# Linear attention feeding a gated product: one DRAM trip for the denominators' reciprocals, and nine pairs alone

## The chip, the cores and the metric

The kernel runs on one core of a Trainium2 chip. The metric is the device time of one execution in microseconds (us), the median of several runs. PE is TensorE, DVE is VectorE, ACT is ScalarE, POOL is GpSimd, SP is SyncE, which here only issues transfers (DMAs).

## The reference

```python
def phi(x):                                    # q, k: 8 batches x 8 heads x 576 x 64
    proj = np.einsum('bhsd,df->bhsf', x, w_phi)            # f = 128
    proj = proj - np.max(np.abs(proj), axis=-1, keepdims=True)
    return np.concatenate([np.exp(proj), np.exp(-proj)], axis=-1)
q_p, k_p = (phi(q), phi(k))
kv = np.einsum('bhsf,bhsd->bhfd', k_p, v)
z = np.sum(k_p, axis=2)
num = np.einsum('bhsf,bhfd->bhsd', q_p, kv)
den = np.einsum('bhsf,bhf->bhs', q_p, z)[..., None] + 1e-06
x = (num / den), heads side by side            # 4608 tokens x 512
out = ((x @ w_a) * (x @ w_b)) @ w_out          # w_a, w_b: 512 x 1536; w_out: 1536 x 512
```

## The kernel before

**Attention** goes over 32 pairs of heads (8 batches of 4 pairs; pair i is written b_pr, with i = 4 b + pr, so pair 8 is 2_0). For a pair, `project` makes the features: PE multiplies q into `pq` (two halves) and k into `pk`; DVE takes the largest magnitude `m` of k's rows and subtracts it (`d`), ACT takes both exponentials (`e`); for q, ACT copies `pq` to `p32`, POOL reduces over partitions (`mb`), DVE subtracts (`p`), ACT exponentiates (`eq`). 64 of a head's 576 keys are left over from the blocks of 128; they are done for two pairs together (`rk`, `e_r`, `m_r`, `d_r`). `kv_products` sums k's features times v into the bank `kv`; `z_products` puts the features' sums over the keys into a third part of the same bank, and `kv_out` copies it out (`back`). `turned_kv` transposes `back` on PE (`pt`) and DVE copies the result out (`kvh`). `num_products` then gives the numerators `pn`, which ACT copies to `x32`, and `den_products` the denominators `pd`. `pd` and `pt` take the same PSUM bank by turns while attention is alone. In `pd` each of four strips of 32 partitions holds 32 equal rows: one half of the times of one head.

**Sums over the keys.** For pairs from `ALONE` on, `summed` has DVE add the key blocks first (`two`, then `z` twice), and `z_products` needs 4 products; for the others it does 20 products on PE over the blocks themselves.

**Denominators.** `den_products` copies `pd` to `dn` and writes one row of each strip to DRAM (`den`). `reciprocals` runs in steps at later turns: read `den` back as 128 x 9 (`r`); add EPS and take the reciprocal on DVE (L306, L307); write it to DRAM (`rec`); read each head's row broadcast to 64 partitions (`rb`); multiply `x32` by `rb` on DVE (L316); write the result to DRAM (`xnorm`).

**The gated product** reads `xnorm`. Its first pass handles 6 of the 12 slices of the hidden dimension in 12 blocks of 384 tokens (`moe_block`; `pa`, `pb` and `po` are its sums, `h` the product of `pa` and `pb`, split in two for accuracy as `hh`, `hl`; `x` is split as `xh`, `xl`). The second pass (`winograd`) handles the rest from the same `xnorm`. The weights come in 64-bit form and are decoded in small steps by ACT and DVE (`w_a`, `w_b`, `w_o`: 18 tiles of 128 x 512, five DVE instructions each, spread over four steps).

**Order.** A planner counts turns, `TURNS` = 4 to a pair. Each unit of a pair is put at a turn: `SPREAD` for the first `ALONE` pairs, `PACKED` after them; the steps of `reciprocals` lie `rec_turns` after the denominators' products. Up to turn `begin` = 4 (`ALONE` + 1) attention is alone with the decoding (0.8 decode steps to a turn); after it there are 2.2 decode steps to a turn, and steps of the gated product run at `PACE0` and then `PACE` to a turn. PE's order of products is fixed as written while this lasts. `behind` and `issue_after` put an instruction behind the last load, or the last subtraction `d`, on its engine; SP issues all loads and stores in one queue, and an instruction that waits there holds up those after it.

Of the kernel before, what the change touches and what calls it, by code (L numbers as in the profile page):

```python
# [9 lines left out]
F32 = mybir.dt.float32  # L10
U32 = mybir.dt.uint32
F32R = mybir.dt.float32r
AF = mybir.ActivationFunctionType
# [5 lines left out]
P = 128  # L19
EPS = 1e-6  # L20


TURNS, ALONE = 4, 8
SPREAD = dict(turned_kv=9, kv_products=5, num_products=10, z_products=6, kv_out=6, den_products=11)
PACKED = dict(summed=2, turned_kv=5, kv_products=3, num_products=7, z_products=3, kv_out=3, den_products=7)
REC_TURNS0, REC_TURNS, X_TURNS = (2, 4, 5, 6, 8, 9), (1, 2, 2, 3, 4, 4), (2, 6)
DECODE_TURN, BLOCK_LAG = 3, 1
DECODE_ALONE, DECODE_BESIDE = 0.8, 2.2
PACE0, PACE, PACE0_TURNS = 0.36, 0.82, 21
# [14 lines left out]
def tile_kernel(ctx, tc, qP, km, kr, vm, vr, w_phi, eye, w_a, w_b, w_out, out):  # L44
# [13 lines left out]
    nc = tc.nc  # L58
    B, NPAIR, _, S = qP.shape
    H = 2 * NPAIR  # L60
    D, F = w_phi.shape
    DM, NT = out.shape
    DF = w_a.shape[0]
    NFULL = S // P
    HALF = S // 2
# [8 lines left out]
    xpool = xstack.enter_context(tc.tile_pool(name="xpool", bufs=1, side="right"))  # L74
    wpool = ctx.enter_context(tc.tile_pool(name="wpool", bufs=1))
    pstack = ExitStack()
    den = [dpool.tile([H, S], F32, name=f"den{b}") for b in range(B)]
    rec = [dpool.tile([H, S], F32, name=f"rec{b}") for b in range(B)]
    xnorm = [dpool.tile([DM, S], F32, name=f"xnorm{b}") for b in range(B)]
    part = dpool.tile([DM, NT], F32, name="part")  # L80
# [40 lines left out]
    def attention_consts(a1):  # L121
        w2 = a1.tile([P, F], F32, name="w2")
        for j in range(2):
            nc.scalar.dma_start(w2[j * D : (j + 1) * D, :], w_phi)
        ident = a1.tile([P, P], F32, name="ident")
        nc.scalar.dma_start(ident, eye)
        busy = a1.tile([P, 2 * S], F32, tag="eq", bufs=2, name="busy")[:, :WARM]
        nc.vector.memset(busy, 0.0)
        warm = duo("warm")
        for _ in range(WARM_TIMES):  # L130
            mm(warm[:, 0, :WARM], busy[:, :P], busy)
        ones = a1.tile([P, 3, D // 2], F32, name="ones")
        nc.vector.memset(ones, 1.0)
        nc.vector.memset(ones[D:, 1], 0.0)
        nc.vector.memset(ones[:D, 2], 0.0)
        return w2, ident, ones

    def split(hi, lo, src, eng_hi, eng_lo):

# [80 lines left out]
    def summed(b, pr, a1, a2, consts, st):  # L220

        u = f"{b}_{pr}"
        e, er = st["e", b, pr], st["er", b, pr // 2]
        two = a1.tile([P, 2, 2, 2 * F], F32, tag="two", name=f"two_{u}")
        ev = e.rearrange("p j c s f -> p j c (s f)")
        nc.vector.tensor_tensor(two, ev[:, :, 0:2], ev[:, :, 2:4], op=ALU.add)
        z = st["z", b, pr] = a2.tile([P, 2, 2 * F], F32, tag="z", bufs=1, name=f"z_{u}")
        nc.vector.tensor_tensor(z, two[:, :, 0], two[:, :, 1], op=ALU.add)
        rows = heads[pr % 2]
        rv = er.rearrange("p j c s f -> p j (c s f)")  # L230
        nc.vector.tensor_tensor(z[rows], z[rows], rv[rows], op=ALU.add)
# [38 lines left out]
    def num_products(b, pr, a1, a2, consts, st):  # L270
        u = f"{b}_{pr}"
        kvh, eq = st["kvh", b, pr], st["eq", b, pr]
        pn = duo(f"pn_{u}")
        for t in range(2):
            for s in range(2):
                for j in range(2):
                    mm(pn[heads[j], t, :HALF], kvh[:, s, heads[j]], eq[:, j, s, times[t]], start=(s == 0), stop=(s == 1))
        x32 = st["x", b, pr] = a2.tile([P, S], F32, tag="x32", bufs=3, name=f"x32_{u}")
        nc.scalar.copy(x32.rearrange("p (t n) -> p t n", t=2), pn[:, :, :HALF])

    def den_products(b, pr, a1, a2, consts, st):
        u = f"{b}_{pr}"
        kvh, eq = st["kvh", b, pr], st["eq", b, pr]
        pd = bank("pt", f"pd_{u}").rearrange("p s f -> p (s f)")
        for s in range(2):
            for j in range(2):
                for t in range(2):
                    mm(pd[strips[2 * j + t], :HALF], kvh[:, 2, strips[2 * j + s]], eq[:, j, s, times[t]], start=(s == 0), stop=(s == 1))
        dn = a2.tile([P, HALF], F32, tag="dn", bufs=1, name=f"dn_{u}")
        nc.scalar.copy(dn, pd[:, :HALF])  # L290
        rows = dn.rearrange("(g r) n -> g r n", r=P // 4)[:, 0]
        nc.sync.dma_start(den[b][2 * pr : 2 * pr + 2].rearrange("h (t n) -> (h t) n", t=2), rows)

    def behind(what, issue):

        with tc.issue_after(what[-1].ins):
            issue()

    def reciprocals(b, pr, a1, a2, st):

        n = 2 * S // P
        hs, rows = slice(2 * pr, 2 * pr + 2), slice(pr * P, (pr + 1) * P)
        r = a1.tile([P, n], F32, tag="rec", bufs=2, name=f"r_{b}_{pr}")
        behind(loads, lambda: nc.sync.dma_start(r, den[b][hs].rearrange("h (a n) -> (h a) n", n=n)))
        yield
        behind(marks, lambda: nc.vector.tensor_scalar_add(r, r, EPS))  # L306
        nc.vector.reciprocal(r, r)  # L307
        yield
        behind(loads, lambda: nc.sync.dma_start(rec[b][hs].rearrange("h (a n) -> (h a) n", n=n), r))
        yield  # L310
        rb = a2.tile([P, S], F32, tag="rb", bufs=1, name=f"rb_{b}_{pr}")
        for j in range(2):
            behind(loads, lambda: nc.sync.dma_start(rb[heads[j]], rec[b][2 * pr + j : 2 * pr + j + 1].broadcast_to([D, S])))
        yield
        x32 = st["x", b, pr]
        behind(marks, lambda: nc.vector.tensor_tensor(x32, x32, rb, op=ALU.mult))  # L316
        yield
        behind(loads, lambda: nc.sync.dma_start(xnorm[b][rows], x32))
        yield

    def attention_steps(pools, consts, st):

        stages, x_first = [], first_block_x()

        def once(f, *args):
            f(*args)
            yield

        def plan(order, unit, turns):
            for t in turns:  # L330
                stages.append((t, order, len(stages), unit))

        for i in range(B * NPAIR):
            b, pr = divmod(i, NPAIR)
            t0 = TURNS * i
            args = (b, pr, *pools, consts, st)
            at = SPREAD if i < ALONE else PACKED
            if i == ALONE - 1:
                at = dict(SPREAD, turned_kv=8, num_products=8, den_products=8)
            units = ((project, 0), (turned_kv, 0), (summed, 0), (kv_products, 0), (num_products, 0), (z_products, 0), (kv_out, 0))  # L340
            units += ((den_products, 0), (load_kq, -5), (load_v, -2))
            for order, (f, t) in enumerate(units):
                if f is not summed or i >= ALONE:
                    plan(order, once(f, *args), [t0 + at.get(f.__name__, t)])
            rec_turns = REC_TURNS0 if i < ALONE - 2 else REC_TURNS
            done = t0 + at["den_products"]
            plan(10, reciprocals(b, pr, *pools, st), [done + t for t in rec_turns])
            if b == 0:
                plan(11, x_first, [done + rec_turns[-1] + t for t in X_TURNS])
            if pr == NPAIR - 1:  # L350
                plan(12, b, [done + rec_turns[-1]])
        stages.sort(key=lambda x: x[:3])
        for turn_, group in itertools.groupby(stages, key=lambda x: x[0]):
            ready = None
            for *_, unit in group:
                if isinstance(unit, int):
                    ready = unit
                else:
                    next(unit, None)
            yield turn_, ready  # L360
# [142 lines left out]
    def first_block_x():  # L503

        for c in range(NCC):
            x32 = x_chunk(0, 0, c, xpool, 2)
            yield
            with tc.issue_after(acts[-1].ins), tc.issue_after(marks[-1].ins):
                x_make(0, 0, c, x32, xpool)
            yield  # L510
# [330 lines left out]
    def first_block(block):  # L841
        next(block)
        for f in range(NFS[0]):
            while (0, f, "b") not in weights:
                yield
            next(block)
            yield
        while (0, NFS[0] - 1, "o") not in weights:
            yield
        yield from block  # L850

    def home(f, nm):
# [4 lines left out]
    begin = TURNS * (ALONE + 1)  # L857
    with ExitStack() as c:
# [7 lines left out]
        decode_steps = placed(load_weights(units, pools[0]))  # L866
        for turn, ready in attention_steps(pools, consts, st):
            if ready is not None:
                at = max(turn + BLOCK_LAG, begin + 1)
                done, blocks[0] = blocks[0], (ready + 1) * S // T1  # L870
                tasks.setdefault(at, []).extend(moe_block(0, j) for j in range(done, blocks[0]))
                if ready == 0:
                    tasks[at][0] = first_block(tasks[at][0])
# [149 lines left out]
```

## Time and profile before

| | us |
|---|---|
| median of 3 runs | 1222.34 (1221.86 to 1228.75) |
| the profiled execution, whole time | 1230.14 |
| its span, first to last instruction | 1228.4 |
| PE busy | 1152.3 (94%) |
| DVE busy | 772.5 (63%) |
| ACT busy | 560.7 (46%) |
| POOL busy | 140.5 (11%) |

The span is what the views divide up; 1.7 us of the execution lie around it. Attention alone fills about the first 120 us, attention beside the gated product the stretch up to 580 us, the rest of the first pass lasts to about 820 us, and the second pass ends the program.

### The profile page before, as it was taken

To read this page: it belongs to the slowest core of one execution; us is meant where nothing else is said; L and a number is where in the kernel's file an instruction comes from. 1 tells how busy PE (TensorE), PEld (TensorE's weight loads), DVE (VectorE), ACT (ScalarE), POOL (GpSimd) and SP (SyncE) were. 2 spreads that over 40 slices of the span, in tenths; PEclk is the share of its full clock that TensorE was granted. 3 is DMA by queue.
4 is the path that set the end of the run, shared out by engine and by line. 5 is a ranking of instruction groups with operands and counts; after the bars stand their busy time and mean duration, and the time that the engine had idled before them with its cause. 6 is when DMAs were issued, how large, how long until landed. Compare 5 with 4: busy or idle time off the path is not lost.

```text
span 1228.4 us, 20607 instructions
## 1 busy us (share of the span) xinstructions
PE 1152.3 (94%) x7974; PEld 1027.5 (84%) x7974; DVE 772.5 (63%) x1411; ACT 560.7 (46%) x1050; POOL 140.5 (11%) x69
## 2 busy tenths in 40 slices
PE   7877886999999999999989999999999999999998
PEld 5544664688878788887989999999999999998997
DVE  6777789355555555554588722527768596867665
ACT  6765565345445444544355322424435353534332
POOL 4432213121212121211000000000000000000000
PEclk9998998899999999999999999999999999999999
DMA  6555544224232232312489410038576776768572
GB/s 203 154 172 162 156 146 141 96 68 127 79 117 93 84 121 65 123 48 82 158 292 312 137 46 25 28 118 308 177 268 213 221 247 215 252 201 284 174 236 97
DMA packets 103074, 191.73 MB, mean 156 GB/s; under 512 B 19520, under 2 KB 54720, under 8 KB 102976
## 3 DMA queue, kind: packets, MB, share of 16 engines
q1 hardware_dynamic: 102672, 190.28, 48.3%
q8 instruction: 63, 1.03, 0.4%
q14 instruction: 35, 0.29, 0.1%
q10 hardware_dynamic: 304, 0.13, 0.0%
HBM read 150.75 MB, written 39.62 MB: 155 GB/s over the span
## 4 chain that ended last, share of the span: by engine, by line
PE 68%; DMA 13%; DVE 12%; ACT 3%; issue 2%; SPq 1%; DVEq 0%; ACTq 0%
PE po L755 10%; PE pa L104 10%; PE pb L104 9%; PE pa L644 9%; PE pb L644 9%; PE po L104 9%; PE kv L104 4%; PE pn L104 3%; DMA rb<-rec 2%; PE pd L104 2%; DMA back_w<-kept_w 2%; DMA x<-xnorm 2%; PE pq L104 2%; DMA den<-dn 2%; DVE d L176 1%
## 5 line engine op out<-in xcount | busy, mean ns | idle before, releaser
L214 POOL PARTITION_ALL_REDUCE mb<-p x64 | 140.2, 2233 | 422.7 <-ACT p L208 329.6
L104 PE MATMUL po<-hh,w_o 128*128 128x384 f32 x576 | 156.8, 345 | 13.4 <-DVE w_o L426 8.6
L104 PE MATMUL pa<-xh,w_a 128*128 128x384 f32 x576 | 162.5, 343 | 0.7 <-DVE h L536 0.7
L104 PE MATMUL pb<-xh,w_b 128*128 128x384 f32 x576 | 158.9, 337 | 1.9 <-ACT o L566 1.7
L104 PEld LDWEIGHTS po<-hh,w_o 128*128 128x128 f32 x576 | 106.5, 192 | 20.6 <-DVE w_o L426 9.4
L104 PEld LDWEIGHTS pa<-xh,w_a 128*128 128x128 f32 x576 | 106.0, 190 | 6.2 <-ACT back L260 2.3
L104 PEld LDWEIGHTS pb<-xh,w_b 128*128 128x128 f32 x576 | 105.3, 188 | 2.6 <-ACT o L566 2.1
L104 PE MATMUL po<-hl,w_o 128*128 128x384 f32 x288 | 97.9, 341 | 1.1 <-DVE hl L141 1.1
L104 PE MATMUL pa<-xl,w_a 128*128 128x384 f32 x288 | 97.3, 338 | 0.0
L104 PE MATMUL pb<-xl,w_b 128*128 128x384 f32 x288 | 96.9, 336 | 0.0
L536 DVE TENSOR_TENSOR h<-pb,h 128x384 f32<-128x384 f32 x72 | 39.6, 550 | 84.2 <-PE pb L104 74.5
L175 DVE TENSOR_REDUCE m<-pk 128x8 f32<-128x1024 f32 x32 | 39.1, 1221 | 79.6 <-PE pk L104 79.5
L140 ACT CAST hh<-h 128x384 fp32r<-128x384 f32 x72 | 36.9, 512 | 111.3 <-DVE h L536 111.1
L755 PE MATMUL po<-hh_s,own_o 128*128 128x384 f32 x288 | 80.3, 336 | 0.3 <-ACT u L743 0.3
L104 PE MATMUL pn<-eq,kvh 128*64 128x288 f32 x512 | 70.1, 417 | 9.2 <-DVE kvh L268 7.9
L104 PE MATMUL kv<-e,v 128*64 128x256 f32 x512 | 66.7, 406 | 8.1 <-ACT back L260 4.6
L104 PEld LDWEIGHTS pn<-eq,kvh 128*64 128x64 f32 x512 | 38.6, 141 | 34.6 <-ACT p L208 7.0
L104 PEld LDWEIGHTS kv<-e,v 128*64 128x64 f32 x512 | 35.5, 143 | 31.4 <-issue 8.5
L755 PE MATMUL po<-hh_w,own_o 128*128 128x384 f32 x216 | 59.2, 334 | 0.0
L104 PE MATMUL pq<-q,w 64*128 64x288 f32 x256 | 48.0, 450 | 11.5 <-ACT p L196 6.8
L216 ACT ACTIVATE eq<-p 128x1152 f32<-128x1152 f32 x32 | 37.3, 1165 | 42.4 <-DVE p L215 37.7
L104 PEld LDWEIGHTS po<-hl,w_o 128*128 128x128 f32 x288 | 55.1, 191 | 1.4 <-DVE hl L141 1.4
(257 smaller groups left out, 2630.0 us busy)
## 6 DMA issues: line engine op xcount, KB each, us to landing
back_s<-kept_s SPq DMA_DIRECT2D x71, 512.0 KB
back_w<-kept_w SPq DMA_DIRECT2D x52, 512.0 KB
q<-in_qP SPq DMA_DIRECT2D x32, 288.0 KB
rb<-rec SPq DMA_DIRECT2D x64, 144.0 KB
xnorm<-x SPq DMA_DIRECT2D x32, 288.0 KB
part<-o SPq DMA_DIRECT2D x48, 192.0 KB
o<-part SPq DMA_DIRECT2D x24, 384.0 KB
out_x<-o SPq DMA_DIRECT2D x48, 192.0 KB
```

Of the source, the lines that this page charges most:

```text
L104: issue = lambda: nc.tensor.matmul(out, w, x, start=start, stop=stop, skip_group_check=True)
L140: (eng_hi.copy if eng_hi is nc.scalar else eng_hi.tensor_copy)(hi, src)
L175: nc.vector.tensor_reduce(out=m, in_=p, op=ALU.max, axis=AX.X, apply_absolute_value=True)
L176: marks.append(nc.vector.tensor_tensor(d, p, m.unsqueeze(3).broadcast_to([P, 2, n, F]), op=ALU.subtract))
L214: nc.gpsimd.partition_all_reduce(mb, p32[:, j], P, bass_isa.ReduceOp.absmax)
L216: nc.scalar.activation(eq[:, :, 0], p32, AF.Exp)
L536: nc.vector.tensor_tensor(h32, pab["b"], h32, op=ALU.mult)
L644: in_turn(lambda: nc.tensor.matmul(acc[to][i], w_, x_, skip_group_check=True, **at), u.startswith("1_0"))
L755: in_turn(lambda: nc.tensor.matmul(acc[m, to], w_, h_, skip_group_check=True, **f), False)
```

## The change

`dn` now takes EPS with its copy out of PSUM (an activation with a bias in place of a copy), and DVE takes the reciprocal of the whole tile `dn`, 128 x 288, in place. One row of each strip goes to DRAM as `rec` and comes back broadcast as `rb`; the trip of `den` out and back, the 128 x 9 tile and its two DVE instructions are gone. The steps lie at other turns: before a pair's `rb` is read, a period of four turns passes in the stretch alone (`REC_TURNS0`), one turn beside the gated product (`REC_TURNS`). `dn` and `rb` get two buffers in place of one. `ALONE` is 9 in place of 8, so that `begin` moves from turn 36 to turn 40, and the first block starts when `x_first` is done. `summed` runs only from pair 15 on (`SUM_FROM`); pairs 8 to 14 do 20 products for `z` in place of 4. `two` shares a buffer with `d`, three early `x32` tiles lie in another pool.

```diff
-TURNS, ALONE = 4, 8
+TURNS, ALONE, SUM_FROM = 4, 9, 15
-REC_TURNS0, REC_TURNS, X_TURNS = (2, 4, 5, 6, 8, 9), (1, 2, 2, 3, 4, 4), (2, 6)
+REC_TURNS0, REC_TURNS1, REC_TURNS, X_TURNS = (1, 3, 7, 10, 10), (1, 3, 6, 8, 8), (1, 2, 3, 5, 6), (5, 8)
+EARLY_X = (0, 2, 4)
...
-        two = a1.tile([P, 2, 2, 2 * F], F32, tag="two", name=f"two_{u}")
+        two = a1.tile([P, 2, 2, 2 * F], F32, tag=f"d{NFULL}", name=f"two_{u}")
...
-        dn = a2.tile([P, HALF], F32, tag="dn", bufs=1, name=f"dn_{u}")
-        nc.scalar.copy(dn, pd[:, :HALF])
-        rows = dn.rearrange("(g r) n -> g r n", r=P // 4)[:, 0]
-        nc.sync.dma_start(den[b][2 * pr : 2 * pr + 2].rearrange("h (t n) -> (h t) n", t=2), rows)
+        dn = st["dn", b, pr] = a2.tile([P, HALF], F32, tag="dn", name=f"dn_{u}")
+        nc.scalar.activation(dn, pd[:, :HALF], AF.Identity, bias=consts[3])
...
-        behind(loads, lambda: nc.sync.dma_start(r, den[b][hs].rearrange("h (a n) -> (h a) n", n=n)))
-        yield
-        behind(marks, lambda: nc.vector.tensor_scalar_add(r, r, EPS))
-        nc.vector.reciprocal(r, r)
-        yield
-        behind(loads, lambda: nc.sync.dma_start(rec[b][hs].rearrange("h (a n) -> (h a) n", n=n), r))
-        yield
-        rb = a2.tile([P, S], F32, tag="rb", bufs=1, name=f"rb_{b}_{pr}")
+        dn = st["dn", b, pr]
+        behind(marks, lambda: nc.vector.reciprocal(dn, dn))
+        yield
+        one = dn.rearrange("(g r) n -> g r n", r=P // 4)[:, 0]
+        behind(loads, lambda: nc.sync.dma_start(rec[b][2 * pr : 2 * pr + 2].rearrange("h (t n) -> (h t) n", t=2), one))
+        yield
+        rb = a2.tile([P, S], F32, tag="rb", name=f"rb_{b}_{pr}")
...
-                if f is not summed or i >= ALONE:
+                if f is not summed or i >= SUM_FROM:
-            rec_turns = REC_TURNS0 if i < ALONE - 2 else REC_TURNS
+            rec_turns = REC_TURNS0 if i < ALONE - 4 else REC_TURNS1 if i < ALONE - 2 else REC_TURNS
...
+        yield
         yield from block
...
-                at = max(turn + BLOCK_LAG, begin + 1)
+                at = max(turn + (BLOCK_LAG if ready else X_TURNS[-1] + 1), begin + 1)
```

DVE's queue around the projection of pair 5 (1_1), in the stretch alone, before (`x32_0_1` and `r_0_2` are of pairs 1 and 2):

```order
L175 TENSOR_REDUCE m_1_1_655<-pk_1_1_645 128x8
L176 TENSOR_TENSOR d_1_1_654<-pk_1_1_645,m_1_1_655 128x1024
L268 COPY kvh_0_3_683<-pt_0_3_679 128x384
L316 TENSOR_TENSOR x32_0_1_460<-x32_0_1_460,rb_0_1_696 128x576
L306 TENSOR_SCALAR r_0_2_699<-r_0_2_699 128x9
L307 RECIPROCAL r_0_2_699<-r_0_2_699 128x9
```

The same place with the change:

```order
L177 TENSOR_REDUCE m_1_1_640<-pk_1_1_630 128x8
L178 TENSOR_TENSOR d_1_1_639<-pk_1_1_630,m_1_1_640 128x1024
L305 RECIPROCAL dn_0_2_616<-dn_0_2_616 128x288
L270 COPY kvh_0_3_667<-pt_0_3_663 128x384
L315 TENSOR_TENSOR x32_0_0_338<-x32_0_0_338,rb_0_0_603 128x576
```

The reciprocal now stands ahead of the copy `kvh` (in the pairs with an even number it stands behind it), the two small instructions are gone, and the multiplication is of one pair earlier.

SP's queue in the same stretch before, with the two trips of pairs 0 and 1:

```order
L309 DMA rec0_76<-r_0_0_449 128x9
L313 DMA rb_0_0_574<-rec0_76 64x576 x2
L292 DMA den0_68<-dn_0_1_498 4x288
L304 DMA r_0_1_577<-den0_68 128x9
L150 DMA k32_1_2_630<-in_km 128x512
```

With the change, from the reads of pair 0's row on:

```order
L312 DMA rb_0_0_603<-rec0_68 64x576 x2
L165 DMA rv_1_2_718<-in_vr 128x256
L308 DMA rec0_68<-dn_0_1_491 4x288
L389 DMA raw_0_2_a_728<-in_w_a 128x1024
L152 DMA k32_1_3_741<-in_km 128x512
L154 DMA q32_1_3_743<-in_qP 128x576
L168 DMA v32_1_2_720<-in_vm 128x512
L312 DMA rb_0_1_722<-rec0_68 64x576 x2
```

A write and the read of the same row stand five rows apart there, where before the read of `den` followed its write at once.

DVE's queue at the last weight tile of the first pass, `w_0_5_o`, before; pair 14 (3_2) has just been projected:

```order
L307 RECIPROCAL r_3_0_2154<-r_3_0_2154 128x9
L215 TENSOR_TENSOR p32_3_2_2111<-p32_3_2_2111,mb_3_2_0_2146 128x576
L228 TENSOR_TENSOR z_3_2_2202<-two_3_2_2200 128x512
L415 TENSOR_SCALAR w_0_5_o_2108<-w_0_5_o_2108 128x512
L231 TENSOR_TENSOR z_3_2_2202<-z_3_2_2202,e_r_3_2_2142 64x512
L417 TENSOR_SCALAR w_0_5_o_2108<-w_0_5_o_2108 128x512
L422 SCALAR_TENSOR_TENSOR w_0_5_o_2108<-raw_0_5_o_2059,w_0_5_o_2108 128x512
L423 TENSOR_TENSOR w_0_5_o_2108<-w_0_5_o_2108,w_0_5_o_2157 128x512
L215 TENSOR_TENSOR p32_3_2_2111<-p32_3_2_2111,mb_3_2_1_2149 128x576
L316 TENSOR_TENSOR x32_3_0_2081<-x32_3_0_2081,rb_3_0_2207 128x576
L426 TENSOR_TENSOR w_0_5_o_2157<-w_0_5_o_2108 128x512
```

With the change, where pair 15 (3_3) has just been projected:

```order
L178 TENSOR_TENSOR d_3_3_2259<-pk_3_3_2250,m_3_3_2260 128x1024
L315 TENSOR_TENSOR x32_3_0_2026<-x32_3_0_2026,rb_3_0_2172 128x576
L305 RECIPROCAL dn_3_1_2234<-dn_3_1_2234 128x288
L421 SCALAR_TENSOR_TENSOR w_0_5_o_2175<-raw_0_5_o_2134,w_0_5_o_2175 128x512
L422 TENSOR_TENSOR w_0_5_o_2175<-w_0_5_o_2175,w_0_5_o_2179 128x512
L270 COPY kvh_3_2_2285<-pt_3_2_2281 128x384
L228 TENSOR_TENSOR two_3_3_2318<-e_3_3_2263 128x1024
L217 TENSOR_TENSOR p32_3_3_2245<-p32_3_3_2245,mb_3_3_0_2271 128x576
L425 TENSOR_TENSOR w_0_5_o_2179<-w_0_5_o_2175 128x512
```

The last weight tile stands one pair later; on PE the first output block `po` of the first block stands one pair later too, behind the transposition of pair 14 in place of pair 13.

## Rows read from the trace of the kernel before

**Rows 1.** Engines by stretch: us, PE, PEld, DVE, ACT, POOL busy, clock, DMA.

```profile
27.85:82.95 55.10, 46.62 (x607) 30.82 (x603) 40.38 (x61) 40.43 (x61) 24.06 (x11) 1.00 0.50 155
82.95:121.37 38.42, 28.21 (x278) 16.44 (x274) 27.78 (x48) 20.09 (x31) 9.17 (x5) 0.87 0.53 165
121.37:217.10 95.73, 71.68 (x553) 54.15 (x549) 80.75 (x132) 54.89 (x88) 22.69 (x10) 0.91 0.48 143
217.10:240.00 22.90, 22.90 (x158) 16.96 (x160) 6.24 (x9) 6.50 (x11) 4.26 (x2) 0.86 0.28 91
```

**Rows 2.** DVE's waits for DMA in the first three stretches: us, times, longest.

```profile
DVE x L316 <- DMA rb<-rec: 8.5, 3, 4.0
DVE r L306 <- DMA r<-den: 3.5, 2, 1.9
...
DVE r L306 <- DMA r<-den: 4.0, 3, 2.1
DVE x L316 <- DMA rb<-rec: 3.7, 2, 3.0
...
DVE x L316 <- DMA rb<-rec: 7.0, 4, 3.0
DVE r L306 <- DMA r<-den: 1.5, 1, 1.5
```

**Rows 3.** Waits of PE over the span: total, times, longest.

```profile
PE kv L104 <- DVE z L231: 8.8, 5, 3.4
PE po L104 <- DVE w_o L426: 8.6, 2, 4.8
PE pn L104 <- DVE kvh L268: 7.9, 6, 2.1
```

**Rows 4.** PE in order of time, attention alone: start, us, instruction, [wait before it].

```profile
52.78 2.16 PE L104 MATMUL pn<-eq,kvh 128*64 128x288 f32 x16
54.87 1.08 PE L104 MATMUL kv<-e,ones 128*32 128x128 f32 x32
...
55.98 1.15 PE L104 MATMUL pd<-eq,kvh 128*32 128x288 f32 x16
...
57.66 1.06 PE L104 MATMUL pk<-w,k 64*128 64x128 f32 x16
```

**Rows 5.** PE in order of time, beside the gated product: last weight, `z` by 4 products.

```profile
217.09 0.69 PE L104 MATMUL po<-hh,w_o 128*128 128x384 f32 x1 [3.74 <-DVE w_o L426]
...
285.43 0.43 PE L104 MATMUL kv<-z,ones 128*32 128x128 f32 x8
285.68 1.15 PE L104 MATMUL pd<-eq,kvh 128*32 128x288 f32 x16
...
366.18 0.42 PE L104 MATMUL kv<-z,ones 128*32 128x128 f32 x8 [1.99 <-DVE z L231]
```

**Rows 6.** DVE in order of time: two small instructions, each with the one behind it.

```profile
45.10 0.18 DVE L306 TENSOR_SCALAR r<-r 128x9 f32<-128x9 f32 x1
45.18 0.68 DVE L422 SCALAR_TENSOR_TENSOR w_a<-raw_a,w_a 128x512 f32<-128x512 uint32 x1
...
59.15 0.22 DVE L307 RECIPROCAL r<-r 128x9 f32<-128x9 f32 x1
59.28 0.37 DVE L415 TENSOR_SCALAR w_b<-w_b 128x512 uint32<-128x512 uint32 x1
```

**Rows 7.** DVE's groups up to 240 us: count, busy us, mean ns, idle before.

```profile
L215 DVE TENSOR_TENSOR p<-p,mb 128x576 f32<-128x576 f32 x31 | 22.9, 740 | 0.1
L316 DVE TENSOR_TENSOR x<-x,rb 128x576 f32<-128x576 f32 x14 | 11.0, 787 | 17.7 <-DMA rb<-rec 17.4 <-issue 0.3
L226 DVE TENSOR_TENSOR two<-e 128x1024 f32<-128x1024 f32 x8 | 9.5, 1194 | 0.0
L228 DVE TENSOR_TENSOR z<-two 128x512 f32<-128x512 f32 x8 | 5.4, 680 | 0.0
L231 DVE TENSOR_TENSOR z<-z,e_r 64x512 f32<-64x512 f32 x7 | 4.8, 680 | 0.1
```

More of the change, by code (lines that the diff above doesn't have):

```diff
@@ L76, in tile_kernel @@
     pstack = ExitStack()
-    den = [dpool.tile([H, S], F32, name=f"den{b}") for b in range(B)]
     rec = [dpool.tile([H, S], F32, name=f"rec{b}") for b in range(B)]
@@ L135, in attention_consts @@
         nc.vector.memset(ones[:D, 2], 0.0)
-        return w2, ident, ones
+        eps = a1.tile([P, 1], F32, name="eps")
+        nc.vector.memset(eps, EPS)
+        return w2, ident, ones, eps
     def split(hi, lo, src, eng_hi, eng_lo):
@@ L277, in num_products @@
                     mm(pn[heads[j], t, :HALF], kvh[:, s, heads[j]], eq[:, j, s, times[t]], start=(s == 0), stop=(s == 1))
-        x32 = st["x", b, pr] = a2.tile([P, S], F32, tag="x32", bufs=3, name=f"x32_{u}")
+        i = b * NPAIR + pr
+        place, bufs = (alone["early"], 2) if i in EARLY_X else (a2, 3)
+        x32 = st["x", b, pr] = place.tile([P, S], F32, tag="x32", bufs=bufs, name=f"x32_{u}")
         nc.scalar.copy(x32.rearrange("p (t n) -> p t n", t=2), pn[:, :, :HALF])
@@ L299, in reciprocals @@
     def reciprocals(b, pr, a1, a2, st):
-        n = 2 * S // P
-        hs, rows = slice(2 * pr, 2 * pr + 2), slice(pr * P, (pr + 1) * P)
-        r = a1.tile([P, n], F32, tag="rec", bufs=2, name=f"r_{b}_{pr}")
-        behind(loads, lambda: nc.sync.dma_start(r, den[b][hs].rearrange("h (a n) -> (h a) n", n=n)))
+        rows = slice(pr * P, (pr + 1) * P)
+        dn = st["dn", b, pr]
+        behind(marks, lambda: nc.vector.reciprocal(dn, dn))
         yield
-        behind(marks, lambda: nc.vector.tensor_scalar_add(r, r, EPS))
-        nc.vector.reciprocal(r, r)
+        one = dn.rearrange("(g r) n -> g r n", r=P // 4)[:, 0]
+        behind(loads, lambda: nc.sync.dma_start(rec[b][2 * pr : 2 * pr + 2].rearrange("h (t n) -> (h t) n", t=2), one))
         yield
-        behind(loads, lambda: nc.sync.dma_start(rec[b][hs].rearrange("h (a n) -> (h a) n", n=n), r))
-        yield
-        rb = a2.tile([P, S], F32, tag="rb", bufs=1, name=f"rb_{b}_{pr}")
+        rb = a2.tile([P, S], F32, tag="rb", name=f"rb_{b}_{pr}")
         for j in range(2):
@@ L505, in first_block_x @@
         for c in range(NCC):
-            x32 = x_chunk(0, 0, c, xpool, 2)
+            with tc.issue_after(loads[-1].ins):
+                x32 = x_chunk(0, 0, c, xpool, 2)
             yield
```

## The prediction

> **What bounds the kernel now.** I read the busy times by stretch first, then the waits of PE and DVE, then both engines in order of time where those waits lie. In all, PE is busy 1152.3 of 1228.4 us, so the end is set by PE's work and by what PE loses. The losses to look for lie ahead of 240 us. While attention is alone (27.85 to 82.95 us) five pairs take 55.10 us, 11.0 each, of which PE is busy 46.62 and DVE 40.38 [rows 1]: neither is full, and DVE stands 12.0 us waiting for the row of denominators (`r`) or of reciprocals (`rb`) to come back from DRAM [rows 2]. The reader should see that PE and DVE wait for each other by turns here: a pair's `m` and `d` on DVE need PE's `pk`, and PE's `pn` needs DVE's `kvh`. In the passage to the gated product (82.95 to 121.37 us) PE is busy 28.21 of 38.42 us, with 7.7 us of such DMA waits on DVE; beside the gated product (to 217.10 us) 71.68 of 95.73 us, with 8.5 us of them, and DVE is busy for 80.75 [rows 1, 2]. [...] That stretch ends with PE waiting for the last weight that DVE decodes, at 217.09 us [rows 5]; DVE's sums `z` and weights are PE's longest waits [rows 3]. From there to 240 us PE has no idle time [rows 1].
>
> So I follow the time at which that last weight is ready. It stands one pair later in the changed order, on DVE and on PE. The pair that PE has then done more is worth 46.62 / 5 = 9.3 us [rows 1]. Equal to before would be 217.1 + 9.3 = 226.4 us.
>
> **The reciprocal's price.** No row shows one of 288 columns; 32 of these now stand on DVE. The one of 9 columns lets the next instruction start after 0.13 us, the addition of 9 columns after 0.08 [rows 6]. The difference over 9 columns is 5.6 ns a column beyond an addition's; at about 1 ns for that (0.74 us for 576 columns with the fixed part [rows 7]) a column takes some 6.6 ns and 288 of them 1.9 us, with the fixed part 1.95 us. Bounds: if all that is extra in the small one is fixed, 288 columns take 0.3 + 0.15 = 0.45 us; if nothing in it is fixed, 288 x 0.13 / 9 = 4.2 us. I take 1.95, an estimate, since the additions of 9 columns show that a fixed part of some 0.07 exists. The two small instructions that go took 0.18 + 0.22 = 0.4 [rows 6], so a pair gains 1.55 us on DVE.
>
> The rows give about 6.6 ns a column. [...]
>
> **Part by part, stretch by stretch.** The trip of `den` and `r` goes, and `rb` is read four turns behind its write, or one beside the gated product; SP's rows between write and read are loads that wait for products long done. I cost the transfers at nothing: DVE's 28.2 us of DMA waits [rows 2] go, and what is late next is DVE itself, whose queue now holds the reciprocal. Queued behind it are, in the odd pairs alone, `kvh`, for which PE's `pn` waits, and everywhere the subtractions `p`, for which ACT's `eq` waits. The bias in ACT's copy of `pd` I cost at nothing, as the same elements pass. SP loses one transfer out and one in to a pair; POOL's queue is not touched.
>
> *Alone.* DVE had 40.38 / 5 = 8.1 us of work a pair, now 8.1 + 1.55 = 9.65, against PE's 9.3. In two pairs the loop runs from the even pair's `m` to the odd pair's `kvh` on DVE, then over PE from `pn` to the end of the next `pk`, 52.78 to 58.72 = 5.9 us [rows 4]. On DVE that is 19.3 less what stands behind the odd pair's `kvh`: a multiplication 0.79, two `p` 1.48 [rows 7] and about half a pair's decoding, some 1.2 by instructions of 0.68 [rows 6], 3.5 in all. 19.3 - 3.5 + 5.9 = 21.7, or 10.8 a pair; before it was 11.0. Six pairs: 65 us, up to 27.85 + 65 = 92.9.
>
> *Passage.* On DVE: 38.42 less 7.7 of DMA waits, less two pairs' `summed` at 1.19 + 0.68 + 0.68 = 2.55 [rows 7], plus two reciprocals at 1.55; on PE plus two pairs' `z`: 1.11 us with 20 products (54.87 to 55.98 [rows 4]) for 0.25 with 4 (285.43 to 285.68 [rows 5]), 0.86 each. That is 30.4 if DVE's part decides and 40.1 if nothing of the waits is won, since PE and ACT wait for each other there too. I take 36: 128.9 us.
>
> *Beside the gated product.* DVE's 80.75 us lose five `summed` (12.8) and gain 5 x 1.55 = 7.8, one early `two` of pair 15 (1.2), and lose 3.2 of the decode steps, which the four more turns alone have done at 0.8 a turn: about 2.6 us at 0.68 an instruction and five instructions to four steps [rows 6]. Sum: 74.3. Of DVE's 15.0 us idle, 8.5 were DMA waits [rows 1, 2]; 6.5 stay, and I add 2 because a DVE with less to do waits more for PE: 82.8. PE's own work there is 71.68 at a clock of 0.91, about 65 at full, plus 5 x 0.86 = 69.5: not the bound, but near enough that little more can be won. The weight is ready at 128.9 + 82.8 = 211.7 us, 14.7 ahead of 226.4.
>
> *Later.* The pairs from 15 on keep `summed`, with the reciprocal now ahead of it. PE waited for `z` five times, two of them after 240 us (366.18 is one [rows 5]); 1.55 more each is 3.1 us. The other fifteen such sums came early enough to show no wait, and I leave them at nothing; what hides them is a step of the gated product on PE between a pair's products. I add 1 us won from less time at the lower clock level. Sum: -14.7 + 3.1 - 1 = -12.6 us. The profiled execution, 1230.1 us, would become 1217.5; it stood 7.8 above the median of the three runs, so against that median the forecast is 1222.3 - 12.6 = **1210 us**.
>
> **Rivals.**
> *The order eats it.* The wait for DMA is only changed into a wait for the reciprocal ahead of `kvh` and `p`. For it: PE already waited 7.9 us for `kvh` [rows 3], and the last weight still stands behind a whole pair's work. Then 6 x 11.0 = 66, 40.1 and 74.3 + 15.0 = 89.3 give 223.3, and with the 3.1 later **1222**. Against it: those waits grew in pairs where DVE had just stood for DMA.
> [...]
> *The reciprocal is dear.* At 4.0 us, near the upper bound, DVE is the bound in every stretch: 13 x 2.05 = 26.7, and `z` comes 2 us later in 17 pairs, of which I count five as unhidden, 10: **1247**, slower than before. It decides from a price of about 2.65 us (12.6 over 18 places is 0.7) and makes it slower by over 1% from 3.3. Against it: the fixed part that the addition of 9 columns shows.
> *The reciprocal is cheap.* At 0.45 us PE is the bound alone: 6 x 9.3 = 55.8 for 65, passage 3 less, beside the gated product 69.5 + 9 = 78.5 for 82.8, nothing late afterwards: 20 us more won, **1190**.
> That the change doesn't do what it says I exclude: the order shows the trip gone and the reads behind.
>
> **How the numbers follow.** Forecast 0.42, its own range 1198 to 1217; the order 0.18; eight cycles 0.12; dear 0.13; cheap 0.15. A measurement of this kernel tells about 1% from no change. Faster by over 1% (under 1210.1): cheap 0.15 and the better part of the forecast 0.30, 0.45. Within 1%: the rest of the forecast 0.12 and the two rivals at 1219 to 1222, 0.29 together with a small part of the edges, 0.41. Slower: 0.14. The range goes from the cheap case to a little beyond the order's, 1190 to 1229, and leaves out the dear one.
>
> **What would show it.** The reciprocals of 128 x 288 at 1.8 to 2.1 us; no wait of DVE for `rb` worth naming; pairs alone 10.5 to 11 us apart, with PE waiting for `kvh` in the odd ones; PE's first `po` waiting for its last weight at 206 to 217 us; 0.86 us more of PE for each of pairs 8 to 14; waits for `z` gone there and longer from pair 15 on. The prediction is wrong if the reciprocal's price is not near 1.95 us, if the first `po` no longer waits and PE is full beside the gated product (then more is won), or if SP's queue holds back loads of k and q, which showed no such wait before.

## The result, and the profile after

| | before | after |
|---|---|---|
| median of 4 runs, us (lowest to highest) | 1223.42 (1221.86 to 1228.75) | 1209.43 (1205.79 to 1214.27) |
| ratio, 95% interval | 1 | 0.9881 [0.9834, 0.9927] |
| profiled execution, us; its span | 1230.1; 1228.4 | 1205.8; 1204.0 |
| TensorE clock, mean of the span | 0.983 | 0.991 |

Faster by 1.2%, with 1210 forecast. The two spans differ by 24.4 us and the medians by 14.0: the profile of before is of a run 6.7 us above its median, that of after of one 3.6 us below. Some 10 us of what the traces show is therefore not the change's, and the text below leans on stretches and medians rather than on the whole spans.

The stretches of after that answer to [rows 1], each ended at the same event: six pairs alone, passage, beside the gated product, and from the last weight to 226.4 us.

```profile
27.54:92.54 65.00, 57.02 (x730) 37.77 (x727) 57.92 (x70) 49.55 (x74) 27.43 (x13) 0.97 0.53 163
92.54:128.05 35.51, 26.35 (x282) 16.34 (x280) 26.41 (x36) 17.71 (x27) 8.99 (x4) 0.90 0.54 165
128.05:213.77 85.72, 72.86 (x734) 57.16 (x730) 74.01 (x109) 54.12 (x85) 21.92 (x10) 0.98 0.50 157
213.77:226.40 12.63, 12.63 (x101) 8.63 (x103) 2.04 (x4) 5.33 (x8) 0.00 (x0) 0.86 0.19 63
```

DVE shows no wait for a DMA of the reciprocals in the first three of them. Before had 25.3 us of such waits up to 217 us:

```profile
DVE x L316 <- DMA rb<-rec: 16.2, 8, 4.0
DVE r L306 <- DMA r<-den: 9.1, 6, 2.1
```

The waits of PE over the span of after, to [rows 3] (total, times, longest):

```profile
PE pn L104 <- DVE kvh L270: 11.6, 5, 3.9
...
PE po L104 <- DVE w_o L425: 5.2, 1, 5.2
...
PE kv L104 <- DVE z L233: 0.8, 1, 0.8
```

PE of after in order of time: an odd pair's `pn`, and the last weight, to [rows 5].

```profile
57.68 2.16 PE L104 MATMUL pn<-eq,kvh 128*64 128x288 f32 x16 [1.75 <-DVE kvh L270]
...
213.77 0.62 PE L104 MATMUL po<-hh,w_o 128*128 128x384 f32 x1 [5.19 <-DVE w_o L425]
```

DVE of after in order of time, ahead of that `pn`. The reciprocal stands between `d` and `kvh`, and the multiplication `x` of an earlier pair behind `kvh`.

```profile
52.71 1.22 DVE L177 TENSOR_REDUCE m<-pk 128x8 f32<-128x1024 f32 x1 [0.42 <-PE pk L104]
54.04 1.23 DVE L178 TENSOR_TENSOR d<-pk,m 128x1024 f32<-128x1024 f32 x1
55.18 1.94 DVE L305 RECIPROCAL dn<-dn 128x288 f32<-128x288 f32 x1
57.04 0.49 DVE L270 COPY kvh<-pt 128x384 f32<-128x384 f32 x1
57.45 1.83 DVE L315 TENSOR_TENSOR x<-x,rb 128x576 f32<-128x576 f32 x1
```

The last weight is ready at 213.77 us, against the 226.4 at which the two kernels would be even: 12.6 us ahead, 14.7 forecast. The rest of the difference between the traces comes later: the second pass begins at 816.35 us before and at 794.03 after, 22.3 us apart. The stretches from the last weight to there, first before, then after:

```profile
217.09:816.35 599.26, 586.39 (x4038) 517.87 (x4038) 317.97 (x575) 262.99 (x489) 72.46 (x34) 0.99 0.35 110
213.77:794.03 580.26, 573.38 (x3950) 510.73 (x3951) 331.83 (x550) 260.37 (x482) 68.87 (x32) 0.99 0.35 111
```

The second is 19.0 us shorter, of which the pair that PE has already done is 9.3. Of the 9.7 us left, 6.0 are idle time of PE (12.9 us before, 6.9 after). Some 3 are clock: in these stretches PE's granted clock stood at 0.50, its lower level, for 13.2 us before and 6.8 after, and at 1.00 otherwise. Work took 1.9 times as long at 0.50: 16 products of `kv` took 3.68 us at 217.70 us in before, 1.95 at 238.37. How much of the 9.7 us belongs to the change is open, since it is of the size of the 10 us by which the two profiled runs stray from their medians.

### The profile page after: what moved, and what is told of

The parts are those of the page before. It is cut to its first block, busy times and chain, and to the rows that moved or that the text cites. A ratio compares the mean times of both kernels' runs of the same rounds, so it can differ in the third digit from the quotient of the medians.

```text
span 1204.0 us, 20915 instructions
## 1 busy us (share of the span) xinstructions
PE 1149.0 (95%) x8198; PEld 1030.4 (86%) x8198; DVE 795.8 (66%) x1359; ACT 565.0 (47%) x1050; POOL 139.3 (12%) x69
## 4 chain that ended last, share of the span: by engine, by line
PE 70%; DVE 10%; DMA 5%; ACT 3%; issue 2%; SPq 0%; ACTq 0%; DVEq 0%
PE po L755 10%; PE pa L104 10%; PE po L104 10%; PE pb L104 10%; PE pa L644 9%; PE pb L644 9%; PE kv L104 4%; PE pn L104 3%; DMA x<-xnorm 2%; PE pd L104 2%; PE pq L104 2%; DMA back_w<-kept_w 1%; PE pk L104 1%; DVE dn L305 1%; DVE h L536 1%
## 5 line engine op out<-in xcount | busy, mean ns | idle before, releaser
L104 PE MATMUL pn<-eq,kvh 128*64 128x288 f32 x512 | 72.0, 426 | 14.5 <-DVE kvh L270 11.6
L305 DVE RECIPROCAL dn<-dn 128x288 f32<-128x288 f32 x32 | 62.2, 1943 | 8.5 <-ACT dn L294 8.5
```

The source lines that it names most:

```text
L104: issue = lambda: nc.tensor.matmul(out, w, x, start=start, stop=stop, skip_group_check=True)
L305: behind(marks, lambda: nc.vector.reciprocal(dn, dn))
```

## Experiments

The change has three parts that can be taken apart: the trip with what belongs to it (reciprocals in the strip tile, the reads later than the writes, and the first block's loads of `x` put behind the last load issued, a line not among those shown), the ninth pair alone, and the sums on VectorE only from the sixteenth pair. Medians are in us; each ratio is to runs of the kernel before on the same chip (medians 1225.0 to 1225.3 there). The result above was measured beside runs of before with a median of 1223.4, so a difference from 1209.43 by medians can be off by one or two us; the ratios allow for that.

**The reads no longer behind the writes.** The changed kernel with one list for all pairs:

```diff
-REC_TURNS0, REC_TURNS1, REC_TURNS, X_TURNS = (1, 3, 7, 10, 10), (1, 3, 6, 8, 8), (1, 2, 3, 5, 6), (5, 8)
+REC_TURNS0, REC_TURNS1, REC_TURNS, X_TURNS = (1, 2, 3, 5, 6), (1, 2, 3, 5, 6), (1, 2, 3, 5, 6), (5, 8)
```

> The change with all three lists of turns set to (1, 2, 3, 5, 6): the row of reciprocals is read one turn behind its write in the stretch alone too. My theory (the gain is DVE's waits for DMA, gone because the read lies a period behind the write): DVE waits for rb again in pairs alone, some 2 to 4 us a pair in six pairs, and the time is 1216 to 1224. The theory that the sums moved to PE gave the gain, and the theory that the ninth pair alone gave it: 1209, as the change.

1214.76 (1213.25 to 1218.12), 0.9919 [0.9901, 0.9937]: some 5 us lost, above the 1209 of two of the theories and a little below the 1216 of mine. But not to a transfer: up to 217 us DVE has no wait for `rb` here either. What moved is the multiplication. DVE in order of time, ahead of an odd pair's `kvh`:

```profile
54.58 1.22 DVE L177 TENSOR_REDUCE m<-pk 128x8 f32<-128x1024 f32 x1
55.90 1.22 DVE L178 TENSOR_TENSOR d<-pk,m 128x1024 f32<-128x1024 f32 x1
57.05 0.75 DVE L315 TENSOR_TENSOR x<-x,rb 128x576 f32<-128x576 f32 x1
57.71 1.95 DVE L305 RECIPROCAL dn<-dn 128x288 f32<-128x288 f32 x1
59.57 0.49 DVE L270 COPY kvh<-pt 128x384 f32<-128x384 f32 x1
```

It stands ahead of `kvh`, and PE's waits for `kvh` are 17.3 us in place of 11.6. On these traces the longer lists pay as a place in DVE's queue, not as cover for the trip to DRAM; no run moves the multiplication by itself.

**The sums back on VectorE from the tenth pair.** The changed kernel:

```diff
-TURNS, ALONE, SUM_FROM = 4, 9, 15
+TURNS, ALONE, SUM_FROM = 4, 9, 9
```

> The change with SUM_FROM 9: pairs 9 to 14 have DVE add the key blocks again and PE does 4 products for z. My theory: DVE, which decides when the last weight of the first pass is ready, gets five times 2.55 us more up to there and PE 0.86 less each: 1215 to 1220. Sums theory: the whole gain goes, 1222 or more. Ninth-pair theory: 1204 to 1209, since PE has 5 us less to do.

1215.76 (1214.41 to 1216.65), 0.9920 [0.9903, 0.9936], within the 1215 to 1220 of my theory: moving the sums is worth 6.3 us within the change by the medians, 4.8 by the ratios, whose intervals overlap.

**The ninth pair by itself.** The kernel before:

```diff
-TURNS, ALONE = 4, 8
+TURNS, ALONE = 4, 9
```

> The kernel before with ALONE 9 and nothing else (two trips, the old turns, sums on DVE from pair 9 on). My theory: nothing that DVE waits for changes, a pair alone costs about what it saves beside the gated product: 1219 to 1227. Ninth-pair theory: 1210. Sums theory: 1221 to 1225.

1210.45 (1209.25 to 1213.20), 0.9883 [0.9868, 0.9898]: one number changed, both trips in place, and as fast as the whole change. My theory, that the gain is the DMA waits removed from DVE, fell here: it was not needed for a gain of this size. PE's waits over its span:

```profile
PE pn L104 <- DVE kvh L268: 8.8, 6, 2.4
PE kv L104 <- DVE z L231: 8.5, 4, 3.5
...
PE po L104 <- DVE w_o L426: 1.1, 1, 1.1
```

Of the three waits in [rows 3] only that for the weight `w_o` has gone, 8.6 to 1.1.

**The trip by itself.** The changed kernel with both other parts taken back:

```diff
-TURNS, ALONE, SUM_FROM = 4, 9, 15
+TURNS, ALONE, SUM_FROM = 4, 8, 8
```

> The change with ALONE 8 and SUM_FROM 8: one trip and late reads alone, without the ninth pair and without the sums moved. My theory: the waits for DMA go and reciprocals come, DVE has about as much to do up to the last weight as before plus 14 x 1.55 = 22 us of work for 28 us of waits gone, so a part of the gain is left: 1214 to 1221. Both other theories: 1223 or more, since the reciprocal only adds work.

1221.27 (1215.06 to 1229.14), 0.9970 [0.9946, 0.9995]: about 4 us, hardly resolved, between the 1214 to 1221 of my theory and the 1223 of the others. The runs that follow fill the other cells, and try what the ninth pair cures.

**Nine pairs alone and the moved sums, two trips.** The kernel before:

```diff
-TURNS, ALONE = 4, 8
+TURNS, ALONE = 4, 9
...
-                if f is not summed or i >= ALONE:
+                if f is not summed or i >= 15:
```

> The kernel before with nine pairs alone and the sums on VectorE only from the sixteenth pair; reciprocals by two trips as before. Decoding theory: until the last w_o weight is ready the kernel is bound by VectorE's work, so taking the three sums of six pairs (pairs 9 to 14) off VectorE makes the weight ready earlier, as it did in the changed kernel, where the same move was worth about 6 us (1215.8 to 1209.4): 1204 to 1207 us. Waits theory (mine until now): with two trips VectorE loses the freed time to its waits for r and rb, so that the sums are free: 1209 to 1212. Third: the products on TensorE cost more than they free: 1213 or more.

1215.03 (1211.98 to 1220.00), 0.9925 [0.9895, 0.9956]: above the 1209 to 1212 expected of the waits theory and far from the 1204 to 1207 of the other. Under two trips and with nine pairs alone the moved sums cost 4.5 us, as the third reading had it: six pairs' products on TensorE are 6 x 0.86 = 5.2 us more. What DVE is spared does not all come back. DVE's waits for DMA up to 217 us, first with nine pairs alone only, then with the sums moved too:

```profile
DVE x L316 <- DMA rb<-rec: 14.4, 9, 5.8
DVE r L306 <- DMA r<-den: 8.8, 6, 3.3
```

```profile
DVE x L316 <- DMA rb<-rec: 17.6, 6, 5.1
...
DVE r L306 <- DMA r<-den: 14.9, 5, 5.0
```

23.2 us became 32.5: DVE has less work here and waits 9.3 us more for the same two transfers. With eight pairs alone the same move lowers these waits (below), so they do not explain the loss by themselves.

**More decoding ahead, before.** The kernel before:

```diff
-DECODE_ALONE, DECODE_BESIDE = 0.8, 2.2
+DECODE_ALONE, DECODE_BESIDE = 0.9, 2.2
```

> The kernel before, eight pairs alone, with 0.9 instead of 0.8 decoding steps for each turn while pairs are alone, so that about three more steps are done when the shared stage begins, as many as nine pairs alone give. Decoding theory (the ninth pair pays because more of the decoding is done when the first block starts): the last w_o weight comes 5 to 9 us earlier, TensorE's 8.6 us of waits for w_o shrink to under 3, and the time is 1213 to 1219 us. Rival (the ninth pair pays because the pair itself is cheaper alone than shared): no change, 1222 to 1227. Third (VectorE is already full in the stage alone): the pairs alone get longer by what the weight gains, 1222 to 1230.

1223.50 (1220.09 to 1228.49), 0.9992 [0.9971, 1.0013]: no change. Yet the last weight did come earlier. The last decoding instruction of `w_o` in before, and here (min/median/max ns, first and last start):

```profile
L426 DVE TENSOR_TENSOR w_o<-w_o x6: 672/678/684, 169.8 to 216.3; 128x512 fp32r<-128x512 f32 x6
```

```profile
L426 DVE TENSOR_TENSOR w_o<-w_o x6: 672/685/991, 163.3 to 208.7; 128x512 fp32r<-128x512 f32 x6
```

It is 7.6 us earlier and PE's waits for `w_o` are 2.9 us in place of 8.6, and the median did not move. So "the ninth pair pays because more is decoded ahead" fell. Where the 7.6 us went can't be read from these two traces: the spans end 6.3 us apart (1228.4 and 1222.1), since the profiled run of before stands some 5 us above the median of its kernel here and this one at its median. How much of the 7.6 us is the edit's is therefore open.

**More decoding ahead, after.** The same edit in the changed kernel:

> The changed kernel with 0.9 decoding steps for each turn alone. Decoding theory: the 5.2 us for which TensorE still waits for the last w_o weight go, 1204 to 1207 us. Rival: VectorE is at 57.9 us of 65.0 in the six pairs alone, so the added steps lengthen that stage instead: 1208 to 1214.

1204.43 (1201.55 to 1208.30), 0.9843 [0.9809, 0.9876]: the 5.2 us wait for the weight is gone and the median is 5.0 lower, as the decoding theory had it, though the interval overlaps that of the changed kernel. That the added steps fit here because DVE no longer stands for DMA is argued, not shown.

**The reciprocal's price taken out.** The changed kernel, where the quotients are not formed:

```diff
-        behind(marks, lambda: nc.vector.reciprocal(dn, dn))
+        behind(marks, lambda: nc.vector.tensor_scalar(dn, dn, 1.0, None, op0=ALU.min))
```

> The changed kernel with the reciprocal of the strip tile replaced by one tensor_scalar of the same tile (a minimum with 1, so that the quotients are not formed): the trip and every wait stay, and the 1.94 us of each reciprocal shrink to about 0.3 us, 1.6 us in each of 32 pairs, some 22 us of VectorE's work before the last w_o weight. If VectorE's work bounds the kernel up to that weight: the wait of 5.2 us for w_o goes and the odd pairs' waits for kvh (11.6 us) fall to about 5, 1198 to 1204 us. If the reciprocals lie in VectorE's idle time: 1207 to 1211.

1195.68 (1192.29 to 1196.34), 0.9764 [0.9734, 0.9793]. In the view of the tile (min/median/max ns) the instruction that is left, and two of PE's waits:

```profile
L305 DVE TENSOR_SCALAR dn<-dn x32: 299/471/1404, 33.0 to 550.0; 128x288 f32<-128x288 f32 x32
```

```profile
PE pn L104 <- DVE kvh L270: 6.3, 5, 2.6
...
PE po L104 <- DVE w_o L425: 1.3, 1, 1.3
```

The time is 2.3 us below the lower end of what was expected if DVE's work is the bound. So the part of the reciprocals' price above that instruction costs the changed kernel 13.8 us (1209.43 less 1195.68) of the 47 us that 32 x 1.47 make on DVE.

**The last two cells.** First the kernel before with the sums moved and eight pairs alone (only the second piece of the edit with two pieces above):

> The kernel before, eight pairs alone and two trips, with the sums on VectorE only from the sixteenth pair. With nine pairs alone this edit cost 4.5 us under two trips (1210.5 to 1215.0). If its sign hangs on the trips alone (under two trips VectorE spends the freed time waiting for r and rb, and TensorE has the extra products to do): 1227 to 1232 us. If it hangs on the number of pairs alone (with eight, VectorE's work for the last w_o weight is what TensorE waits 8.6 us for): 1216 to 1221.

1214.49 (1210.78 to 1217.22), 0.9908 [0.9883, 0.9932]. Both readings on record missed; with eight pairs alone the moved sums are worth 10.7 us even under two trips. PE's waits here, to [rows 3]:

```profile
PE pn L104 <- DVE kvh L268: 6.3, 4, 2.1
...
PE po L104 <- DVE w_o L426: 2.4, 1, 2.4
...
PE kv L104 <- DVE z L231: 1.6, 2, 0.8
```

The waits for `z` and for `w_o`, 17.4 us in [rows 3], are 4.0. DVE's waits for DMA up to 217 us fell too, from 25.3 to 20.9:

```profile
DVE x L316 <- DMA rb<-rec: 13.1, 9, 3.7
DVE r L306 <- DMA r<-den: 7.8, 5, 2.4
```

Then the changed kernel with eight pairs alone:

```diff
-TURNS, ALONE, SUM_FROM = 4, 9, 15
+TURNS, ALONE, SUM_FROM = 4, 8, 15
```

> The changed kernel whole, but with eight pairs alone. One trip with the sums on VectorE lost 5.5 us by this (1215.8 to 1221.3), two trips lost 14.8 (1210.5 to 1225.3). If the ninth pair and the trip are worth their sums apart: 1215 to 1224 us. If the moved sums are what makes the ninth pair unneeded (VectorE's work before the last weight is then short enough with eight): 1208 to 1212.

1203.29 (1198.85 to 1205.83), 0.9814 [0.9785, 0.9843]: below both expectations, and faster than with nine. PE shows no wait at all for `z` or for `w_o` here, and for `kvh` this:

```profile
PE pn L104 <- DVE kvh L270: 8.0, 5, 2.4
```

The eight cells, as medians with the ratio to before:

| | sums on DVE | sums from the sixteenth pair |
|---|---|---|
| two trips, eight alone | 1225 (before), 1 | 1214.5, 0.9908 |
| two trips, nine alone | 1210.5, 0.9883 | 1215.0, 0.9925 |
| one trip, eight alone | 1221.3, 0.9970 | 1203.3, 0.9814 |
| one trip, nine alone | 1215.8, 0.9920 | 1209.4, 0.9881 (after) |

No part has a worth of its own. The ninth pair gives 14.7 us in before and costs about 6 in the changed kernel; the moved sums give 10.7 in before, 18.0 with one trip and eight alone, and cost 4.5 with two trips and nine. What holds in the table: where one of the ninth pair and the moved sums is in place, the other gives less or costs, with one trip and with two; and the moved sums are worth more with one trip (18.0 and 6.3) than with two (10.7 and -4.5). That both cure DVE's lateness for `z` and the last weight is not shown: the ninth pair alone leaves the waits for `z` at 8.5 us of 8.8, and more decoding took off most of the waits for `w_o` and gained nothing.

A part of these differences is TensorE's clock. The granted clock of each cell, as a mean over its runs, in the order of the table:

| | sums on DVE | sums from the sixteenth pair |
|---|---|---|
| two trips, eight alone | 0.984 | 0.988 |
| two trips, nine alone | 0.989 | 0.985 |
| one trip, eight alone | 0.982 | 0.990 |
| one trip, nine alone | 0.981 | 0.989 |

A thousandth of it is at most 1.2 us of PE's work in 1210 us, so the step from 0.984 to 0.989 is, as an estimate, up to 6 of the ninth pair's 14.7 us. Why the clock is higher in some cells is not taken apart by any run.

**The reciprocal behind `kvh`.** The changed kernel with 0.9 decoding steps, and:

```diff
-REC_TURNS0, REC_TURNS1, REC_TURNS, X_TURNS = (1, 3, 7, 10, 10), (1, 3, 6, 8, 8), (1, 2, 3, 5, 6), (5, 8)
+REC_TURNS0, REC_TURNS1, REC_TURNS, X_TURNS = (2, 3, 7, 10, 10), (2, 3, 6, 8, 8), (1, 2, 3, 5, 6), (5, 8)
```

> The changed kernel with 0.9 decoding steps for each turn alone (1204.4 us) and each reciprocal one turn later while pairs are alone, so that it stands behind the copy kvh of the next pair instead of ahead of it. If the reciprocal's price reaches TensorE through kvh: TensorE's 13.0 us of waits for kvh fall to 3 to 6 and the time to 1196 to 1201. If the price is VectorE's total work: the wait moves to the weights or the p tiles and the time stays at 1203 to 1206.

1196.48 (1193.02 to 1199.33), 0.9770 [0.9746, 0.9794], the fastest kernel here that does the whole work, 8 us below the same without the move. The time is as expected, the sign that was to go with it is not: PE's waits for `kvh`, first without and then with the move,

```profile
PE pn L104 <- DVE kvh L270: 13.0, 6, 3.3
```

```profile
PE pn L104 <- DVE kvh L270: 10.6, 8, 2.1
```

fell by 2.4 us only. The stretch up to 217 us of the two in the same order:

```profile
0.00:217.00 217.00, 186.04 (x2050) 132.38 (x2051) 178.36 (x240) 142.79 (x215) 70.47 (x37) 0.97 0.52 170
```

```profile
0.00:217.00 217.00, 189.29 (x2116) 138.04 (x2117) 183.82 (x246) 147.37 (x224) 75.15 (x39) 0.99 0.54 175
```

PE has done 66 matmuls more by then, with 3.3 us more of busy time. The rest is clock, 0.97 and 0.99 as means of this stretch. In the traces of before and after the clock stood at 0.50 in pieces of 3.4 us, once in one of 13.7; the two means make, as an estimate from these, four pieces of 3.4 us in the first and one in the second, 10.2 us less at 0.50, 5.1 us of work. The longest waits, 3.3 and 2.1 us, went with them; that the shorter waits are why the clock stayed up is argued, not shown.

**Ten pairs alone.** The changed kernel with 0.9 decoding steps and:

```diff
-TURNS, ALONE, SUM_FROM = 4, 9, 15
+TURNS, ALONE, SUM_FROM = 4, 10, 15
```

> The changed kernel with 0.9 decoding steps for each turn alone (1204.4 us) and ten pairs alone. If a pair is as such cheaper alone than beside the block (the ninth gave 5.5 to 14.8 us): 1192 to 1200. If the ninth paid because the first block had waits for weights to lose, and these are gone now (no wait for w_o is left): 1203 to 1210, the tenth pair gives nothing or costs the time for which TensorE idles in a pair alone, about 1.5 us, and the block's work at the end.

1208.54 (1207.51 to 1212.95), 0.9868 [0.9844, 0.9892]: 4 us lost. A pair is not as such cheaper alone. In the six pairs alone of after PE idles 8.0 of 65.0 us, 1.3 a pair; from the last weight to 226.4 us it idles not at all. PE's waits for `z` are 3.8 us here and 1.1 in the same kernel with nine. That accounts for part of the 4 us; the rest is open, and the intervals of the two ratios overlap.

## Why the prediction was right, point by point

**The reciprocal's price**: 1.95 us estimated from two instructions of 9 columns, 1.94 measured in all 32. With the fixed part that makes 6.6 ns a column, as worked out. That it came so close is partly luck: the rows that it was worked out from are given to 0.01 us, and 0.01 us more or less in nine columns is 0.3 us in 288.

**Alone** 65 us forecast, 65.0 measured. PE waits for `kvh` in pairs 1 and 3 of this stretch (2.4 and 1.75 us), not in pair 5; that is about half of its 8.0 us of idle time. **Passage** 36 and 35.5. The 7.7 us of DMA waits that went into the lower bound there are 4.7: one wait of 3.0 us, ahead of an instruction that reaches across 82.95 us, stands in two of the stretches of [rows 2], so that their sum is 25.3 us and not 28.2, and the bound 33.4 us and not 30.4. **Beside the gated product** 82.8 and 85.7: the term for DVE's work was right (74.3 forecast, 74.01 busy), but 11.7 us stayed idle where 8.5 were allowed. Up to the last weight the sum was 2.1 us too hopeful.

**Later** is the step that failed. It put 3.1 us lost on the waits for `z` and 1 us won on the clock, 2.1 us lost together. No run shows that 1 us by itself; what the traces show behind the weight is the 13.2 and 6.8 us at a granted clock of 0.50. Between the two traces 9.7 us were won behind the weight, 6.0 of them idle time of PE and some 3 clock. "1.55 more each is 3.1 us" for the waits for `z`: they fell, from 2.8 to 0.8 us behind the weight and from 8.8 to 0.8 over the span. I had followed DVE's DMA waits only up to 217 us. From there to 600 us before had these, and after this one:

```profile
DVE x L316 <- DMA rb<-rec: 28.3, 18, 4.6
...
DVE r L306 <- DMA r<-den: 11.0, 3, 6.9
```

```profile
DVE x L315 <- DMA rb<-rec: 7.9, 3, 5.6
```

So 31.4 us of DVE's waits went there against 17 x 1.55 = 26.4 us of reciprocals, and the balance that I forecast did not turn against `z`. That these waits held the sums back is not shown: with a ninth pair alone and both trips in place PE has no wait for `z` after 217 us either. That 1209.4 came out beside 1210 is in part luck. The sum was worked out on the profiled run of before, and trace against trace it says 1217.5 us; the profiled run of after took 1205.8, 11.7 less. It is the medians, which lie 10 us closer together than the traces, that agree with it.

**The attribution.** Up to the weight the steps added up, but they were read as the price of a queue freed from DMA. The table corrects that: the kernel before reaches 1210.5 with a ninth pair alone and 1214.5 with the moved sums alone, both trips kept. With those two in place the trip and its lists are worth 5.6 us (1215.0 to 1209.4), an amount that the intervals of the two ratios do not separate, and inside it stand 13.8 us of reciprocals. My account credited the ninth pair with the 9.3 us of PE's work in a pair and never asked what it gives without the rest.

**The rivals.** "The order eats it" needed 11.0 us a pair alone and 223.3 us for the weight: 10.8 and 213.77 were measured. "Dear" fell with 1.94 us. The chance of 0.12 for "eight cycles" and its place at 1219 among the forecasts rest on a reciprocal of 2.47 us, which no run shows: the 32 took 1.939 to 1.953 us. "Cheap" was forecast at 20 us below the forecast; with the instruction at a median of 0.47 us the measured step is 13.8, and PE still waits 6.3 us for `kvh`, which that account had at nothing.

## What to carry to other kernels

When a change bundles several parts, price each of them alone on the kernel before: here one number gave the whole gain, and the same number costs in the company of the other two. Taking transfers out of an engine's queue has to be priced with the work put in their place and with where that work stands: here the reciprocals took back 13.8 us, and the order of DVE's queue (some 5 us for the multiplication, 8 for the reciprocal) was worth as much as the trip. Compare medians before explaining a difference between two traces. And follow a kind of wait to the end of its life, not to the end of the stretch in which it was found.

## What the runs showed of the hardware that was not expected

DVE's `x` multiplications, 128x576 with two operands, became slower up to 217 us at their new places. Before and after (count, busy us, mean ns):

```profile
L316 DVE TENSOR_TENSOR x<-x,rb 128x576 f32<-128x576 f32 x13 | 10.3, 789 | 16.4 <-DMA rb<-rec 16.2 <-issue 0.3
```

```profile
L315 DVE TENSOR_TENSOR x<-x,rb 128x576 f32<-128x576 f32 x13 | 13.6, 1052 | 0.0
```

The one at 57.45 us in after took 1.83 us, and GpSimd was at work then:

```profile
55.25 4.26 POOL L216 PARTITION_ALL_REDUCE mb<-p  x2 [5.61 <-ACT p L210]
```

The reciprocal at 55.18, with one operand, kept its 1.94 us through the first half of it. Of the 13, the six that took 1.0 to 1.85 us all ran wholly while GpSimd was at work, but four more that did so as well took 0.74 to 0.78, so that GpSimd's work is not shown to be the cause by itself. The one shown lost 1.1 us (1.83 less the 0.74 of the fastest of its kind), about half the 2.1 us of one GpSimd instruction there. 13 x 0.26 = 3.4 us went that way, which the prediction had not counted.

ACT's copy of `pd` with a bias is no copy in price: 397 ns before, 500 after, for the same 128x288. The prediction had put the bias at nothing.

```profile
L290 ACT COPY dn<-pd 128x288 f32<-128x288 f32 x13 | 5.2, 397 | 2.6 <-PE pd L104 2.4 <-ACT back L260 0.2
```

```profile
L294 ACT ACTIVATE dn<-pd,eps 128x288 f32<-128x288 f32 x14 | 7.0, 500 | 1.8 <-PE pd L104 0.9 <-DMA rv<-in_vr 0.4 <-DMA rb<-rec 0.4
```
